# Windowed attention and a gated convolution block on one core: dense stages regrouped from 12 spans of 384 tokens to 9 of 512

## The chip, the core and the metric

One Trainium2 chip, one of its cores. A core has five engines that run their own instruction queues: TensorE (PE in the profile, with its weight loads shown apart as PEld), VectorE (DVE), ScalarE (ACT), GpSimd (POOL) and SyncE (SP), which here only issues transfers (DMA). The engines wait for each other on semaphores. Matrix products go into PSUM, here eight tiles of 128 x 512 float32; everything else lies in SBUF. The metric is the device time of one execution in microseconds, the median of several runs. The profiler gives one execution with every instruction.

## The reference

Eight sequences of 576 tokens, 8 heads of 64. Attention looks at the last 64 tokens only; then a block with a convolution over three neighbouring tokens of a sequence and a sigmoid gate:

```python
scores = scale * np.matmul(q, k.transpose(0, 1, 3, 2))
mask = (rel >= 0) & (rel < window)                  # window = 64
attn = softmax(np.where(mask, scores, -1e9))        # + 1e-9 in the divisor
x = matmul(attn, v)  ->  [8, 576, 512]
h = np.maximum(x @ w_in, 0.0)                       # 512 -> 1024
for k in range(3):
    conv_out += conv_w[k] * hp[:, k:k + S, :]       # hp: h with a zero row at both ends
gate = 1.0 / (1.0 + np.exp(-conv_out))
out = (h * gate) @ w_out                            # 1024 -> 512
```

Inputs q, k, v are float32; the three weights come as float64. All 8 x 576 = 4608 tokens are treated as one row of tokens, cut at the sequence edges only where the window or the convolution asks for it.

## The kernel before

**Tiling.** A span `u` is `NX` = 6 x 64 = 384 tokens, 12 spans. Channels lie on the 128 partitions: 4 tiles of the model width (`NC`), 8 of the inner width (`NF`). Each float32 operand of a dense product is split into a high and a low part in float32r, and each product is three matmuls (high x high, low x high, high x low).

**Attention of a span.** `softmax` works in groups of four blocks of 64 tokens (`NB` = 4), three groups to a span. A group has score matmuls (`qk`, L356) into the two `sc` tiles; `row_max` (L363) on DVE, which adds the mask and finds the maximum; eight `exps` (L373) on ACT; the reciprocal (L379) and `normalise` (L384) on DVE or POOL. The probabilities are then transposed into `ub`: for the first two spans (`BY_PE` = 2) by PE (`transpose_pe` L390, `untile` L395 on ACT), later by DVE (L411) and 12 small transfers per half of a span (`place`, L423). `values` (L495) multiplies them by v for one of four channel tiles into one of the two `acc` tiles; `split_hi` (L499, ACT) and `split_lo` (L502, DVE) write the parts `xh` and `xl`. q, k and v each have one buffer, refilled (L236, L242) when the previous span's products have read it.

**Dense stages of a span.** For each of 8 tiles `f`: `mm1` (L515), 12 matmuls of 384 columns into an `acc` tile, and `relu` (L534 or L538, ACT) into `hbuf`. `hbufs` are two tiles that hold all 8 relu results of a span each. `carry` (L525, POOL) copies the last two columns of the previous span, which the convolution needs. For each pair of tiles: `conv_mid` (L544, ACT), `conv_side` (L551, DVE) for the two neighbours, `sig` (L558, ACT), `gate` (L563, DVE), `gate_hi` (L567, ACT) and `gate_lo` (L571, DVE) into a ring of three `gh`/`gl` tiles. `mm2` (L580) adds, for each `f`, three matmuls into each of the four `po` tiles, which `copy` (L620, L622) brings to `ot` and a transfer (L626; L617 and L624 in the last span) to memory.

**Filler columns.** A sequence of 576 is one and a half spans. Where it ends, in the middle of a span or at its edge, `hbuf` keeps a zero column (L529) between the sequences (`gap_of`), so that the convolution runs over the whole width at once; with the neighbour's column the width is 386 (`NG`) in most spans and 384 in every third but the last. Filler columns go through `mm2` and out to memory, and are dropped on the host.

**The order.** Every piece of work goes into a list by `at(t, engine, cost, ...)`, with a due time `t` in steps (one step: one tile `f`), a cost in microseconds and the keys that it reads and writes. `START` holds the due times, `queued` plays the list on the costs, gives each engine the ready work that is due first, and so fixes the order of each engine's instructions in advance. On the chip each engine then keeps that order. Where PE would wait in the first 110 us, `queued` puts in warm-up matmuls (`keep_busy`, L214). Weights are converted from float64 bits (`to_f32`, L250 to L256; L271 to L274) in the same list, on ACT, DVE and POOL.

Of the kernel before, what the change touches and what calls it, by code (L numbers as in the profile page):

```python
# [15 lines left out]
P = 128  # L16
W = 64
# [5 lines left out]
NT = 6  # L23
NX = NT * W
NU = B * S // NX
NG = NX + 2
NC = DM // P
NF = DFF // P
BY_PE = 2
NB = 4  # L30
NBU = 2 * NT // NB
# [3 lines left out]


LAST = NU - 1


def gap_of(u):  # L40

    return {0: 0, 1: NX // 2, 2: NX}[u % 3]


def width_of(u):
    return NX if u % 3 == 2 and u != LAST else NG

# [11 lines left out]
def queued(works, fill=None):  # L59
# [80 lines left out]
    "v0": -45.616,  # L140
    "pv0": -37.371,
    "conv": -174.861,
    "bits": ((-210.989, -90.898), (-76.132, -86.24)),
    "qk1": -82.37,
    "lag": (5.734, 4.983, 5.01, 5, 4.601, 6.631),
    "mid": (0.325, 6.316, 0.269, 99),
    "v1": -1.517,
    "qk2": -29.766,
    "qk0": (-93.532, -87.041, -82.642),
    "ex0": (-76.037, -72.861, -50.81),  # L150
    "sc1": (-59.709, -43.924, -30.076),
    "ex1": (-36.764, -20.322, -18.147),
    "mask": -51.623,
    "sig": ((5.726, 6.552, 8.72, 10.544), (1.673, 4.482, 8.678, 7.763), (4.834, 5.504, 8.278, 8.811), (4.046, 6.806, 8.285, 10.314)),
    "in": (-91.819, -70.332, -46.356, -13.522, -9.317),
    "out": (5.121, 7.311, 7.45, 11.284),
# [13 lines left out]
def attention_moe(ctx: ExitStack, tc: tile.TileContext, q, k, v, w_in, conv_w, w_out, out):  # L170
# [9 lines left out]
    xh, xl = many(2, [P, NC, NX], F32R, "xh"), many(2, [P, NC, NX], F32R, "xl")  # L180
    hbufs = many(2, [P, NF, NG + 2], F32, "hbuf")
# [9 lines left out]
    ss = many(NBU, [P, NB, 2, P], F32, "s")  # L191
    nms, sms, rs = (many(NBU, [P, 2 * NB], F32, n) for n in ("nm", "sm", "r"))
    cs = many(2, [P, 2, NG], F32, "c")
    ghs, gls = many(3, [P, 2, NG], F32R, "gh"), many(3, [P, 2, NG], F32R, "gl")
# [14 lines left out]
    def keep_busy(n, key):  # L209
        tile = {"sc": sc, "acc": acc, "po": po}[key[0]][key[1]]  # L210

        def do():
            for _ in range(n):
                nc.tensor.matmul(tile[:, 400:], spare, spare[:, :112], start=True, stop=True)  # L214
# [439 lines left out]
    for u in range(NU):  # L654
        n0 = NF * u
        moe(u)
        if u + 1 == NU:
            break
# [92 lines left out]
```

## Time and profile before

| What | us |
|---|---|
| median of 3 runs | 520.48 |
| lowest and highest of them | 519.96, 521.10 |
| the profiled execution | 519.87 |
| its span, first to last instruction | 517.9 |
| busy in the span: PE / DVE / ACT / POOL | 508.0 / 372.4 / 382.8 / 85.4 |

The rows of the profile are read so: engine, line of the kernel, operation, written tile <- read tiles, shapes, count, then busy time and mean nanoseconds of one, then the idle time of the engine before them and what ended it. In timelines and in the chain of waits the first two numbers are start and length in microseconds. In the table of stretches each engine has its busy time and its count of instructions; the three last columns are the granted TensorE clock (1.00 is full), the busy share of the transfer engines and GB/s. A float32 matmul that isn't float32r shows as two rows in the counts (the 576 calls of `values` are 1152 rows).

### The profile page before, as it was taken

The numbers are of one execution on the slowest core, as the hardware profiler recorded it, in microseconds if no ns is written. First come the engines' busy times: TensorE is split into PE (matmuls) and PEld (weight loads), VectorE is DVE, ScalarE is ACT, GpSimd is POOL, SyncE is SP. The second block draws the span as 40 slices with busy tenths as digits, with TensorE's granted clock in tenths as the row PEclk, the third lists the DMA queues.
The fourth block names the chain that finished last, engine by engine and source line by source line (L and its number), as shares of the span: only waits on it lengthen the run. The fifth ranks groups of instructions, "written<-read, shape, count | busy, mean of one in ns | idle before, by whom it ended". The sixth has DMA issues, their size and how long they took to land.

```text
span 517.9 us, 14661 instructions
## 1 busy us (share of the span) xinstructions
PE 508.0 (98%) x5742; PEld 488.4 (94%) x5742; DVE 372.4 (72%) x1084; ACT 382.8 (74%) x1015; POOL 85.4 (16%) x186
## 2 busy tenths in 40 slices
PE   9899899999999999999999999999999999999996
PEld 8788899999999999999899999899899999999996
DVE  4799998986787785766668877677677578554550
ACT  5989797979995894894796895795795696444440
POOL 7123131003030120130121130130130021000000
PEclk9999999999999999999999999999999999999999
DMA  8974923152382461462272451362272043010011
GB/s 294 380 274 171 350 80 117 62 176 76 127 291 69 145 218 47 138 208 66 96 255 60 161 202 49 123 234 55 86 260 65 3 153 121 1 62 2 0 62 61
DMA packets 29460, 69.95 MB, mean 135 GB/s; under 512 B 5712, under 2 KB 17616, under 8 KB 29392
## 3 DMA queue, kind: packets, MB, share of 16 engines
q1 hardware_dynamic: 29392, 69.03, 39.3%
q8 instruction: 45, 0.74, 0.6%
q14 instruction: 23, 0.19, 0.1%
HBM read 47.73 MB, written 9.47 MB: 110 GB/s over the span
## 4 chain that ended last, share of the span: by engine, by line
PE 82%; DVE 9%; DMA 5%; ACT 1%; issue 1%; SPq 1%; ACTq 0%
PE po L580 38%; PE acc L515 33%; PE acc L495 6%; PE sc L356 5%; DMA q<-in_q_dram 2%; DVE s L363 2%; DMA bits<-in_w_out_dram 1%; DVE s L384 1%; DVE T L252 1%; DVE T L256 1%; DMA k<-in_k_dram 1%; DVE c L563 1%; DVE wil L274 1%; DVE xl L502 1%; SPq L236 1%
## 5 line engine op out<-in xcount | busy, mean ns | idle before, releaser
L580 PE MATMUL po<-gh,woh 128*128 128x386 f32 (+1 forms) x384 | 132.4, 345 | 0.0
L515 PE MATMUL acc<-xh,wih 128*128 128x384 f32 x384 | 130.7, 340 | 0.6 <-ACT hbuf L534 0.6
L580 PE MATMUL po<-gh,wol 128*128 128x386 f32 (+1 forms) x384 | 130.0, 339 | 0.0
L580 PE MATMUL po<-gl,woh 128*128 128x386 f32 (+1 forms) x384 | 129.7, 338 | 0.1
L515 PE MATMUL acc<-xh,wil 128*128 128x384 f32 x384 | 129.0, 336 | 0.3 <-issue 0.3
L515 PE MATMUL acc<-xl,wih 128*128 128x384 f32 x384 | 128.8, 335 | 0.0
L551 DVE SCALAR_TENSOR_TENSOR c<-hbuf,cw,c 128x386 f32<-128x386 f32 (+1 forms) x192 | 111.9, 633 | 22.5 <-ACT c L544 22.4
L373 ACT ACTIVATE s<-s,nm 128x96 f32<-128x96 f32 (+2 forms) x288 | 105.1, 368 | 3.4 <-DVE nm L363 3.2
L580 PEld LDWEIGHTS po<-gh,woh 128*128 128x128 f32 x384 | 72.2, 188 | 2.9
L515 PEld LDWEIGHTS acc<-xh,wih 128*128 128x128 f32 x384 | 72.1, 188 | 2.7 <-ACT hbuf L534 1.1
L580 PEld LDWEIGHTS po<-gl,woh 128*128 128x128 f32 x384 | 72.4, 188 | 0.4 <-DVE gl L571 0.4
L515 PEld LDWEIGHTS acc<-xh,wil 128*128 128x128 f32 x384 | 72.1, 188 | 0.5 <-issue 0.5
L580 PEld LDWEIGHTS po<-gh,wol 128*128 128x128 f32 x384 | 72.2, 188 | 0.0
L515 PEld LDWEIGHTS acc<-xl,wih 128*128 128x128 f32 x384 | 72.1, 188 | 0.0
L563 DVE TENSOR_TENSOR c<-c,hbuf 128x772 f32<-128x772 f32 (+1 forms) x48 | 47.0, 982 | 31.2 <-ACT c L558 30.8
L571 DVE TENSOR_TENSOR gl<-c,gh 128x772 fp32r<-128x772 f32 (+1 forms) x48 | 51.8, 1082 | 22.1 <-ACT gh L567 21.8
L384 POOL TENSOR_TENSOR s<-s,r 128x768 f32<-128x768 f32 x27 | 40.4, 1496 | 152.1 <-DVE r L379 138.8
L363 DVE CUSTOM_DVE_ANT_0 s<-sc,mask 128x96 f32<-128x96 f32 (+2 forms) x272 | 51.9, 257 | 16.8 <-PE sc L356 16.8
L373 ACT ACTIVATION_READ_ACCUMULATOR s<-s,nm 128x1 f32 x288 | 54.6, 190 | 0.0
L558 ACT ACTIVATE c<-c 128x772 f32<-128x772 f32 (+1 forms) x48 | 40.6, 847 | 18.8 <-DVE c L551 18.6
L567 ACT CAST gh<-c 128x772 fp32r<-128x772 f32 (+1 forms) x48 | 40.0, 834 | 18.4 <-DVE c L563 13.7
L544 ACT ACTIVATE c<-hbuf,cw 128x386 f32<-128x386 f32 (+1 forms) x96 | 53.5, 608 | 0.0
(63 smaller groups left out, 551.9 us busy)
## 6 DMA issues: line engine op xcount, KB each, us to landing
v<-in_v_dram SPq DMA_DIRECT2D x24, 768.0 KB, 6.4
ub<-T SPq DMA_DIRECT2D x240, 48.0 KB, 1.9
k<-in_k_dram SPq DMA_DIRECT2D x22, 448.0 KB, 6.2
q<-in_q_dram SPq DMA_DIRECT2D x22, 384.0 KB, 7.0
out_dram<-T SPq DMA_DIRECT2D x8, 772.0 KB, 3.8
bits<-in_w_in_dram SPq DMA_DIRECT2D x8, 512.0 KB, 6.1
bits<-in_w_out_dram SPq DMA_DIRECT2D x8, 512.0 KB, 6.6
out_dram<-T SPq DMA_DIRECT2D x3, 768.0 KB, 4.6
```

The lines of the kernel that those rows point to most:

```text
L363: nc.vector.tensor_tensor_reduce(out=ss[b][:, i, h, o:n], in0=banks_of(u, b)[h][:, i * P + o:i * P + n], in1=mask[m][:, o:n], scale=-0.125 ...
L373: nc.scalar.activation(x, x, AF.Exp, bias=nms[b][:, e], scale=-1.0, accum_out=sms[b][:, e])
L384: on.tensor_tensor(sv, sv, rs[b].unsqueeze(2).broadcast_to([P, 2 * NB, n]), ALU.mult)
L495: nc.tensor.matmul(acc[bank(("v", u, c))][h * D:(h + 1) * D, t * W:(t + 1) * W], vs[:, c, t, h], ub[g][:, 2 * p:2 * p + 2, 2 * t + h], sta ...
L515: nc.tensor.matmul(acc[bank(("m", u, f))][:, :NX], w[:, f, c], x[u % 2][:, c], start=(c == 0 and j == 0), stop=(c == NC - 1 and j == 2))
L544: nc.scalar.activation(cs[i % 2][:, a, :n], hbufs[u % 2][:, f, 1:1 + n], AF.Copy, scale=cw[:, 1, f:f + 1])
L551: nc.vector.scalar_tensor_tensor(c, hbufs[u % 2][:, f, e:e + n], cw[:, e, f:f + 1], c, op0=ALU.mult, op1=ALU.add)
L558: nc.scalar.activation(c, c, AF.Sigmoid)
L563: nc.vector.tensor_tensor(c, c, hbufs[u % 2][:, 2 * i:2 * i + 2, 1:1 + n], ALU.mult)
L567: nc.scalar.copy(ghs[ring(u, i)][:, :, :n], cs[i % 2][:, :, :n])
L571: nc.vector.tensor_tensor(gls[ring(u, i)][:, :, :n], cs[i % 2][:, :, :n], ghs[ring(u, i)][:, :, :n].bitcast(F32), ALU.subtract)
L580: nc.tensor.matmul(po[o][:, :n], w[:, f, es], x, start=(f == 0 and j == 0), stop=(f == NF - 1 and j == 2))
```

## The change

- The dense stages go by 9 spans of 512 tokens (`NM` = 2 x 256, `PER` = 2), attention by 18 units of 256 tokens (`NX` = 4 x 64, `NA`). A unit has two groups of four blocks instead of a span's three; the softmax tiles become a ring of three (`NS`).
- Units 0 to 3 (before: spans 0 and 1) are transposed by PE; for units 0 to 3 (before: spans 0 to 2) `normalise` runs on DVE.
- `values` fills an `acc` tile with two channel tiles of 256 tokens, so there are 36 such jobs instead of 48.
- No zero columns: `conv_side` leaves out the column of a neighbour that belongs to another sequence, by cutting the instruction at that place (`spans`). A span is 512 wide, shifted by one column; the last span is 514 and its second product goes in two parts (`parts`), 258 columns into `po` and 256 into halves of the `sc` tiles.
- `hbufs` (two spans of 8 tiles) become `hs`, a ring of `NH` = 5 pairs of tiles.
- `place` moves one group (12 transfers of 32 KB) instead of half a span (12 of 48 KB).
- Costs and due times in `START` are new.

```diff
-NT = 6
+T = B * S
+NT = 4
 NX = NT * W
-NU = B * S // NX
-NG = NX + 2
+NA = T // NX
...
-BY_PE = 2
 NB = 4
-NBU = 2 * NT // NB
+NBU = 2
+NS = 3
+BY_PE = 4
+ON_DVE = 4
+PER = 2
+NU = NA // PER
+LAST = NU - 1
+NM = PER * NX
+NW = NM + 2
+NH = 5
...
-    xh, xl = many(2, [P, NC, NX], F32R, "xh"), many(2, [P, NC, NX], F32R, "xl")
-    hbufs = many(2, [P, NF, NG + 2], F32, "hbuf")
+    xh, xl = many(2, [P, NC, NM], F32R, "xh"), many(2, [P, NC, NM], F32R, "xl")
+    hs = many(NH, [P, 2, NW + 2], F32, "h")
...
+    def ring_of(u, b):
+        return (NBU * u + b) % NS
...
     def values(u, c):
-        g, p = divmod(c, 2)
-        for t in range(NT):
-            for h in range(2):
-                nc.tensor.matmul(acc[bank(("v", u, c))][h * D:(h + 1) * D, t * W:(t + 1) * W], vs[:, c, t, h],
-                                 ub[g][:, 2 * p:2 * p + 2, 2 * t + h], start=True, stop=True)
+        for p in range(2):
+            for t in range(NT):
+                for h in range(2):
+                    nc.tensor.matmul(acc[bank(("v", u, c))][h * D:(h + 1) * D, p * NX + t * W:p * NX + (t + 1) * W],
+                                     vs[:, 2 * c + p, t, h], ub[c][:, 2 * p:2 * p + 2, 2 * t + h], start=True, stop=True)
...
     def mm1(u, f, half):
         for c in (2 * half, 2 * half + 1):
             for j, (w, x) in enumerate(((wih, xh), (wil, xh), (wih, xl))):
-                nc.tensor.matmul(acc[bank(("m", u, f))][:, :NX], w[:, f, c], x[u % 2][:, c],
+                nc.tensor.matmul(acc[bank(("m", u, f))], w[:, f, c], x[u % 2][:, c],
                                  start=(c == 0 and j == 0), stop=(c == NC - 1 and j == 2))
...
+    def slot(u, i):
+        return (NF // 2 * u + i) % NH
+
+    def carry(u, i):
+        h = hs[slot(u, i)]
         if u == 0:
-            nc.gpsimd.memset(hbuf[:, fs, :2], 0.0)
+            nc.gpsimd.memset(h[:, :, :2], 0.0)
         else:
-            e = NX if (u - 1) % 3 == 2 else NX + 1
-            nc.gpsimd.tensor_copy(hbuf[:, fs, :2], hbufs[(u - 1) % 2][:, fs, e:e + 2])
...
+            nc.gpsimd.tensor_copy(h[:, :, :2], hs[slot(u - 1, i)][:, :, NM:NM + 2])
...
+    def spans(u, e):
+
+        n, t0, res = width_of(u), u * NM - 1, [0]
+        for j in range(n):
+            if 0 < t0 + j < T - 1 and (t0 + j) % S == (0 if e == 0 else S - 1):
+                res += [j, j + 1]
+        res.append(n)
+        return [(x, y) for x, y in zip(res[::2], res[1::2]) if y > x]
...
+    def parts(u, o):
+
+        if u != LAST:
+            return [(0, NM, po[o][:, :NM], halves_of("po", o))]
+        n = NM // 2
+        return [(0, n + 2, po[o][:, :n + 2], halves_of("po", o)),
+                (n + 2, NW, sc[o // 2][:, o % 2 * n:(o % 2 + 1) * n], halves_of("sc", 0)[o // 2:o // 2 + 1])]
...
-                at(t + 0.05, "SP", 2.1, lambda g=g, i=i: place(g, i), r=[("T", g)], w=[("u", g, i)], mb=0.15)
+            at(t + 0.05, "SP", 1.35, lambda i=i: place(b, i), r=[("T", b)], w=[("u", b, i)], mb=0.1)
...
+    "qk": ((-198.384, -170.949), (-193.671, -162.337), (-154.854, -108.704), (-106.623, 1.483), (-6.498, -3.826), (1.331, 4.543), (-0.713, -0.42), (3.501, 3.738)),
+    "ex": ((-164.895, -164.822), (-138.633, -119.099), (-52.881, -37.596), (2.064, 5.523), (1.401, -2.24), (5.799, 5.838), (-0.443, 0.159), (4.214, 4.945)),
+    "pv": ((-139.987, -153.554), (-84.882, -86.539), (1.278, 4.685), (5.77, 6.895), (4.8, 6.129), (7.71, 7.584), (3.763, 3.861), (7.594, 7.387)),
```

381 lines of the change are left out of this document (160 added, 221 removed), and 4 rows, old and new, of the table START.

## The prediction

> **What bounds the kernel now.** I read the page first: shares of the engines, the slices, the chain that ended last.
>
> ```profile
> span 517.9 us, 14661 instructions
> PE 508.0 (98%) x5742; PEld 488.4 (94%) x5742; DVE 372.4 (72%) x1084; ACT 382.8 (74%) x1015; POOL 85.4 (16%) x186
> ...
> PEclk9999999999999999999999999999999999999999
> ...
> PE 82%; DVE 9%; DMA 5%; ACT 1%; issue 1%; SPq 1%; ACTq 0%
> ```
>
> TensorE (PE) is busy for 98% of the span at the full granted clock, and 82% of the chain lies on it. A busy matmul row isn't a full array, so I went on to the table of stretches, for whether other engines are close behind, and to PE's timeline for the first dense matmul.
>
> ```profile
> 34.90:67.00 32.10, 30.53 (x487) 27.86 (x485) 31.34 (x94) 28.82 (x71) 10.06 (x19) 1.00 0.69 257
> 340.00:380.00 40.00, 40.00 (x481) 38.68 (x480) 28.66 (x89) 30.42 (x83) 6.51 (x12) 1.00 0.38 126
> ...
> 34.88 0.42 PE L515 MATMUL acc<-xh,wih 128*128 128x384 f32 x1
> ...
> 513.50 0.34 PE L580 MATMUL po<-gl,woh 128*128 128x386 f32 x1
> ```
>
> The columns are the stretch, its length, then busy time of PE, PEld, DVE, ACT and POOL. In the steady part VectorE (28.66 of 40) and ScalarE (30.42) have a quarter of their time free, while PE has none. From 34.88, the first dense matmul, to 513.50, the last one, lie 478.6 us in which PE hardly stops. So the time is a start of 34.9, plus 478.6 of PE work, plus 4.4 of result copies and transfers up to 517.9. The profiled execution took 519.87, 2.0 beyond its span; the median of the three runs is 520.48. My sum is made against 519.87. About 0.2% (1 us) is what a measurement of this kernel can tell from no change.
>
> **The dense matmuls (the main term).** What one costs is read from the chain in order of time (start, length, what).
>
> ```profile
> 482.12 2.10 PE acc L515 x12
> ...
> 496.89 16.96 PE po L580 x96
> ```
>
> ```profile
> L515 PE MATMUL acc<-xh,wih 128*128 128x384 f32 x384 | 130.7, 340 | 0.6 <-ACT hbuf L534 0.6
> L580 PE MATMUL po<-gh,woh 128*128 128x386 f32 x288 | 99.2, 344 | 0.0
> L580 PE MATMUL po<-gh,woh 128*128 128x384 f32 x96 | 33.2, 346 | 0.0
> ...
> L515 PEld LDWEIGHTS acc<-xh,wih 128*128 128x128 f32 x384 | 72.1, 188 | 2.7 <-ACT hbuf L534 1.1
> ```
>
> From one to the next it is 2.10 / 12 = 175 ns for a first product (384 columns) and 16.96 / 96 = 176.7 ns for a second one (386). There are 3 x 384 of each: 1152 x 0.175 + 1152 x 0.1767 = 405.2 us. The change keeps the columns (it drops the fillers: 9 x 386 + 3 x 384 = 4626 become 4610 per weight tile) and cuts the instructions: 9 spans x 96 = 864 first products of 512, 8 x 96 = 768 second ones of 512, and 192 of about 257 in the last span, whose 514 columns don't fit a po tile of 512.
>
> How much of the 175 ns goes by the instruction? No row shows another width of this kind of matmul. A weight load is busy for 188 ns although pairs follow each other every 175, so about 13 ns of each load lie beyond the step from pair to pair; I take this as the hand-over that each instruction pays once. The rest is 162 / 384 = 0.422 ns a column (0.424 for the second). Then 512 columns take 229 and 230 ns and 257 take 122: 864 x 0.229 + 768 x 0.230 + 192 x 0.122 = 198.0 + 176.7 + 23.4 = 398.0, that is -7.2 us. One end: all of it goes by columns, 512 take 233 ns, and only the fillers are saved, -0.7. The other end is a line through the nearest narrow row, the warm-up matmuls:
>
> ```profile
> 12.04 3.60 PE L214 MATMUL acc<-spare 128*128 128x112 f32 x30
> ```
>
> These take 120 ns at 112 columns, so (175 - 120) / 272 = 0.20 ns a column, 201 ns at 512, 149 at 257, and some -47 us. I don't believe it: a 112-column matmul is more likely paced by its weight load of 128 columns than by itself. I take 229.
>
> The Trainium skill, "TensorE: Matmul & The Clock Gate", section "Back-to-back issue gap", gives N/2.4 + 2.5 ns for a warm isolated gap: 162.5 at 384, where this trace has 175, and 216 at 512. An estimate by that page alone would make the saving of fixed time 480 fewer instructions x 2.5 ns = 1.2 us, which speaks against the change; the trace's 12 ns more are not explained by it.
>
> **Attention on PE.** The work per token stays, its grouping changes.
>
> ```profile
> 31.78 1.62 PE L495 MATMUL acc<-ub,v 128*64 128x64 f32 x48
> ...
> 39.25 1.04 PE L390 MATMUL po<-ident,s 128*128 128x128 f32 x8
> ```
>
> ```profile
> 404.48 0.33 PE L580 MATMUL po<-gl,woh 128*128 128x384 f32 x1
> 404.74 1.62 PE L495 MATMUL acc<-ub,v 128*64 128x64 f32 x48
> 406.29 1.00 PE L356 MATMUL sc<-k,q 64*32 64x96 f32 x64
> 407.21 0.44 PE L580 MATMUL po<-gh,woh 128*128 128x384 f32 x1
> 407.50 0.34 PE L580 MATMUL po<-gh,wol 128*128 128x384 f32 x1
> ```
>
> (a) Four units of 256 are transposed by PE instead of two of 384: 8 groups, not 6. Four of them, not two, come after the first dense matmul: 2 more x 1.04 = +2.1. Those before it displace warm-up matmuls, at nothing. (b) Scores: 36 groups of about 0.95 as before, 32 rather than 30 behind the start, +2; values: the first 128 of 1152 instructions rather than 96 come before it, -1.0; a DVE transpose and a placing fall away for units 2 and 3. Since a group of unit 2 can be computed before the start, as the plan's due times have it, I take +0.7 together. (c) Each change between dense and small matmuls costs PE 0.26 - 0.175 going in and 0.29 - 0.175 coming out, 0.2 us. The value products stand in blocks of 48 (two together); behind the start there are 1056 / 48 = 22 such blocks. After, 32 products make 16 blocks if each pair stays together, as their due times lie 0.1 and 0.2 of a step apart, 32 if none does: -1.2 to +2.0; I take -1.2.
>
> **Vector and scalar work** is the same per column in fewer, longer instructions; the cuts at the sequence edges add 7 edges x 2 sides x 8 tiles = 112 small VectorE instructions. Both lie in the 10 of 40 us that VectorE has free. If that cover goes (34.90 to 67.00, where DVE is busy for 31.34 of 32.10), each costs its time.
>
> **The ring of five** makes a relu wait until the pair five before has been gated. Before, all 8 tiles of the previous span stay. Run-ahead is longest at the start:
>
> ```profile
> 34.88:66.77 31.89, 21.78 (x114) 19.47 (x114) 1.00 0.69 258
> ...
> 34.88:66.77 31.89, 1.83 (x2) 1.00 0.69 258
> ```
>
> The first row counts first products, the second the gate multiplications in the same stretch: 114 x 384 columns, as many as 85 x 512, 7.1 tiles or under 4 pairs; the ring holds 5. Cost nothing; if gating stood still for 10 us more, the ring would end first.
>
> ```profile
> L384 POOL TENSOR_TENSOR s<-s,r 128x768 f32<-128x768 f32 x27 | 40.4, 1496 | 152.1 <-DVE r L379 138.8 <-ACT xh L499 10.7 <-ACT c L544 2.5
> L525 POOL COPY hbuf<-hbuf 128x4 f32<-128x4 f32 x44 | 21.7, 493 | 181.4 <-ACT hbuf L538 95.2 <-ACT hbuf L534 86.1
> ```
>
> The carry on GpSimd now guards a slot that the next pair overwrites; it is a 0.5 us copy that can queue behind a 1.5 us normalisation, but is due some two tiles (over 10 us) ahead.
>
> **The start.** The first dense matmul now needs 512 tokens, i.e. four groups of scores instead of three, and values of two units that share one v buffer.
>
> ```profile
> 19.96 0.92 PE L495 MATMUL acc<-ub,v 128*64 128x64 f32 x24
> ...
> 23.04 0.33 SPq L242 DMA_DIRECT2D v<-in_v_dram  x1
> ```
>
> ```profile
> 0.00:34.88 34.88, 15.23 (x77) 1.00 0.86 310
> ...
> v<-in_v_dram SPq DMA_DIRECT2D x24, 768.0 KB, 6.4
> ...
> L499 ACT CAST xh<-acc 128x384 fp32r<-128x384 f32 x48 | 22.4, 476 | 17.8 <-PE acc L495 17.4
> L502 DVE TENSOR_TENSOR xl<-acc,xh 128x384 fp32r<-128x384 f32 x48 | 26.2, 555 | 8.8 <-ACT xh L499 7.6
> ```
>
> The 77 rows are exponentials and their sums on ScalarE: 38, almost five groups of eight, were done by 34.88, and four are needed after. Values of unit 0 around 20 to 22, its buffer reloaded (6.4), values of unit 1 at 28 to 30, a split of 512 columns ((0.476 + 0.555) x 1.33 = 1.4): 31 at the earliest. One group later at ScalarE's pace (15.23 / 38 x 8 = 3.2, with copies some 4): 39. I take 34.9, no change, between 31 and 39.
>
> **The end**: the last bank is again copied in two pieces, so 4.4 stays.
>
> Sum: -7.2 + 2.1 + 0.7 - 1.2 = -5.6; 519.87 - 5.6 = **514.3 us**.
>
> **Rivals.**
> 1. *The time goes by columns.* -0.7 in place of -7.2: 520.8, no change. For it: no row shows another width. Against it: the 13 ns of the weight load. Chance 0.10. By the rule of the Trainium skill named above ("TensorE: Matmul & The Clock Gate", 2.5 ns fixed) the time would come out here too, 0.5 lower.
> 2. *SyncE's queue becomes the bound: slower.* Placing a group issues 12 small transfers, whatever its length.
>
> ```profile
> 305.50 12.65 SPq L423 DMA_DIRECT2D ub<-T  x18
> ...
> ub<-T SPq DMA_DIRECT2D x240, 48.0 KB, 1.9
> k<-in_k_dram SPq DMA_DIRECT2D x22, 448.0 KB, 6.2
> ...
> 330.41 0.33 SPq L236 DMA_DIRECT2D k<-in_k_dram  x1
> ...
> L373 ACT ACTIVATE s<-s,nm 128x96 f32<-128x96 f32 x240 | 86.9, 366 | 0.2
> L373 ACT ACT_TABLE_LOAD x18 | 23.1, 1283 | 4.3 <-DVE nm L363 4.1
> L411 DVE STREAM_TRANSPOSE T<-s 128x768 f32<-128x768 f32 x20 | 19.4, 971 | 3.4 <-POOL s L384 3.3
> ```
>
> 12.65 / 18 = 0.70 us each, 8.4 a group. After, 28 groups issue 336 (of 32 KB), 48 in a dense span of about 52 us: 34 us of SP's time, before 17 of 40. The scores of a span's second unit are due 4.2 steps into it and its values at 7.4: 3.2 steps of 52 / 8 = 6.5, 20.6 us. Eight exponentials with a table load 2.9 + 1.3 = 4.2, normalising 1.5, transposing 1.0, two placings 16.9, landing 1.9: 25.5. It decides if an issue takes over about 0.50 us. The following first products then find no input, and PE's order is fixed: if half of the 4.9 us shows in each of 8 spans, +20, **534**. If the issue goes by bytes (0.47), 19.9 fits. A load of 448 KB that issues in 0.33 speaks against a cost by bytes; later dense work queued ahead of the values can absorb some. Chance 0.13.
> 3. *A late start.* First products at 41 in place of 34.9, because loads and weight conversions compete with the fourth group: 520.4. Against it: five groups were done by then before. Chance 0.10.
> 4. *More gain.* A start at 31 and whole pairs: down to 507, chance 0.09; a matmul halfway between my 229 ns and the 201 of the line through the warm-up row, 215, takes 1632 x 0.014 = 23 more off: 491, chance 0.03.
>
> **How the numbers follow.** Forecast 508 to 518.5, chance 0.55. Rival 2 and the far part of 4 (0.16) stay out of the range, the others are in: 507 to 523. Rivals 1 and 3 lie around the time before: of each 0.02 is faster, 0.06 within 0.2%, 0.02 slower. Faster by over 0.2%: 0.55 + 0.12 + 0.04 = 0.71. Within: 0.12. Slower: 0.13 + 0.04 = 0.17.
>
> **What would show it.** Twelve first products in 2.75 us in the chain (2.80 says rival 1); the first dense matmul between 31 and 39; PE without gaps to the end; 16 blocks of 64 value matmuls. Waits of value products for "ub", and SP's queue full, say rival 2. I am wrong if PE's rows after 60 us show idle time in every span.

## The result and the profile after

The changed kernel took **536.61 us** (median; 534.59 to 538.55) beside 520.79 us for the kernel before on the same chip: a ratio of 1.031 with a 95% interval of 1.026 to 1.035, slower. 514.3 was forecast, within 507 to 523. The profiled execution took 537.26 us, 17.4 more than the 519.87 against which the sum was made.

The page of the kernel after (span; busy time by engine; granted clock by slice; the chain that ended last, by engine):

```profile
span 535.5 us, 13610 instructions
...
PE 509.1 (95%) x5180; PEld 418.7 (78%) x5180; DVE 368.5 (69%) x1096; ACT 375.9 (70%) x932; POOL 76.6 (14%) x122
...
PEclk8999999999899999999999998999999999999999
...
PE 72%; DVE 12%; DMA 4%; SPq 4%; ACT 4%; issue 3%; POOL 0%; ACTq 0%; POOLq 0%
...
ub<-T SPq DMA_DIRECT2D x336, 32.0 KB, 1.9
```

PE was busy for 98% of a span of 517.9 before, now for 95% of 535.5, and its share of the chain fell from 82 to 72%. In its place stand DMA, SyncE's queue (SPq, which issues the transfers) and "issue", time in which an engine waits for nothing that the profile shows. The placing transfers (ub<-T) rose from 240 to 336, each two thirds as large. What PE waited for is told by its table of waits (tile and line that waited, releaser: us in all, times, longest):

```profile
PE acc L452 <- DMA ub<-T: 8.5, 4, 3.1
PE sc L339 <- issue: 4.6, 4, 2.2
...
PE acc L452 <- issue: 0.6, 1, 0.6
```

Value products waited four times, 8.5 us, for the placing transfers. Score products stood still four times, 4.6 us, without a releaser. (Waits for loads of q, not shown, lie before the first dense product.) Here is one of each in PE's timeline (start, length, what, count, the idle time before), with SyncE's queue beside the first:

```profile
115.01 16.45 SPq L392 DMA_DIRECT2D ub<-T  x24
```

```profile
128.08 0.64 PE L339 MATMUL sc<-k,q 64*32 64x96 f32 x32
129.17 0.69 PE L452 MATMUL acc<-ub,v 128*64 128x64 f32 x16 [0.46 <-DMA ub<-T]
132.96 0.56 PE L452 MATMUL acc<-ub,v 128*64 128x64 f32 x5 [3.10 <-DMA ub<-T]
```

```profile
326.24 0.96 PE L339 MATMUL sc<-k,q 64*32 64x96 f32 x61
329.40 0.53 PE L339 MATMUL sc<-k,q 64*32 64x96 f32 x3 [2.19 <-issue]
329.86 0.80 PE L552 MATMUL po<-gh,woh 128*128 128x512 f32 x1
330.45 0.63 PE L552 MATMUL po<-gh,wol 128*128 128x512 f32 x1
330.88 0.63 PE L552 MATMUL po<-gl,woh 128*128 128x512 f32 x1
...
332.58 0.47 PE L552 MATMUL po<-gh,woh 128*128 128x512 f32 x1
```

SyncE issues 24 transfers from 115.01 to 131.46, 0.69 us each though they carry 32 KB and not 48; the value products that need the last of them start at 132.96. The second pause has no such cause, and the dense products behind it follow each other at 427 ns (330.45, 330.88): six steps from 329.86 to 332.58 take 2.72 us where 233 ns each would be 1.40. The granted clock by stretch shows the two places where that happened (length, busy time by engine, PEclk):

```profile
100.00:140.00 40.00, 34.29 (x366) 27.88 (x365) 30.87 (x97) 34.31 (x94) 6.25 (x6) 0.91 0.46 128
140.00:300.00 160.00, 155.76 (x1676) 126.19 (x1682) 106.58 (x343) 109.66 (x266) 20.20 (x22) 1.00 0.40 123
300.00:340.00 40.00, 37.81 (x389) 30.32 (x367) 26.02 (x89) 27.70 (x75) 5.84 (x6) 0.96 0.50 146
```

The start, the end, and the pace of the dense products, from timeline and chain (in the chain's row: start, length, line, count):

```profile
38.12 0.47 PE L477 MATMUL acc<-xh,wih 128*128 128x512 f32 x1
...
529.52 0.28 PE L552 MATMUL sc<-gl,woh 128*128 128x256 f32 x1
```

```profile
417.03 5.61 PE acc L477 x24
...
501.24 2.82 PE po L552 x12
```

So the 17.4 us are: start +3.2 (38.12 against 34.88), end +1.6 (6.0 after the last matmul against 4.4), waits for ub +8.5, pauses without releaser +5.2 (4.6 of scores, 0.6 of values), slow clock twice 1.3. That is 21.1; the remainder, -3.7, is what the regrouping of the small products and the dense steps save less what the transposes add. The dense products, from which -7.2 were expected, saved next to nothing: 5.61 / 24 = 233.7 ns a step in the row above. On the mean over the kernel after, slow clock aside, 864 x 233.4 + 768 x 233.0 + 192 x 119.5 ns = 403.5 us, where 1152 x 174.8 + 1152 x 176.3 ns = 404.5 us stood before: about -1 us.

### The profile page after: what moved, and what is told of

The parts are those of the page before. It is cut to its first block, busy times and chain, and to the rows that moved or that the text cites. A ratio compares the mean times of both kernels' runs of the same rounds, so it can differ in the third digit from the quotient of the medians.

```text
span 535.5 us, 13610 instructions
## 1 busy us (share of the span) xinstructions
PE 509.1 (95%) x5180; PEld 418.7 (78%) x5180; DVE 368.5 (69%) x1096; ACT 375.9 (70%) x932; POOL 76.6 (14%) x122
## 4 chain that ended last, share of the span: by engine, by line
PE 72%; DVE 12%; DMA 4%; SPq 4%; ACT 4%; issue 3%; POOL 0%; ACTq 0%; POOLq 0%
PE po L552 30%; PE acc L477 27%; PE acc L452 5%; PE sc L339 5%; SPq L392 4%; DVE c L515 3%; PE sc L552 2%; DMA q<-in_q_dram 2%; ACT s L357 2%; DVE s L346 2%; PE acc L205 2%; DVE gl L535 2%; DVE c L527 1%; DMA bits<-in_w_in_dram 1%; DVE T L241 1%
## 5 line engine op out<-in xcount | busy, mean ns | idle before, releaser
L515 DVE SCALAR_TENSOR_TENSOR c<-h,cw,c 128x512 f32<-128x512 f32 (+29 forms) x256 | 115.9, 517 | 34.5 <-ACT c L499 34.5
L477 PE MATMUL acc<-xl,wih 128*128 128x512 f32 x288 | 114.4, 397 | 0.0
L477 PE MATMUL acc<-xh,wih 128*128 128x512 f32 x288 | 114.0, 396 | 0.0
L477 PE MATMUL acc<-xh,wil 128*128 128x512 f32 x288 | 113.7, 395 | 0.0
L552 PE MATMUL po<-gh,woh 128*128 128x512 f32 (+1 forms) x288 | 112.4, 390 | 0.2 <-issue 0.2
L552 PE MATMUL po<-gh,wol 128*128 128x512 f32 (+1 forms) x288 | 111.4, 387 | 0.0
L552 PE MATMUL po<-gl,woh 128*128 128x512 f32 (+1 forms) x288 | 110.8, 385 | 0.0
L346 DVE CUSTOM_DVE_ANT_0 s<-sc,mask 128x96 f32<-128x96 f32 (+2 forms) x280 | 54.2, 258 | 33.5 <-PE sc L339 33.3
L535 DVE TENSOR_TENSOR gl<-c,gh 128x1024 fp32r<-128x1024 f32 (+1 forms) x36 | 44.6, 1248 | 18.0 <-ACT gh L531 17.8
L527 DVE TENSOR_TENSOR c<-c,h 128x1024 f32<-128x1024 f32 (+1 forms) x36 | 47.7, 1324 | 13.1 <-ACT c L522 13.0
L499 ACT ACTIVATE c<-h,cw 128x512 f32<-128x512 f32 (+1 forms) x72 | 47.9, 714 | 3.7 <-DVE gl L535 3.5
```

Source lines behind the costliest of these rows:

```text
L346: nc.vector.tensor_tensor_reduce(out=ss[ring_of(u, b)][:, i, h, o:n], in0=banks_of(u, b)[h][:, i * P + o:i * P + n], in1=mask[m][:, o:n], ...
L477: nc.tensor.matmul(acc[bank(("m", u, f))], w[:, f, c], x[u % 2][:, c], start=(c == 0 and j == 0), stop=(c == NC - 1 and j == 2))
L499: nc.scalar.activation(cs[i % 2][:, a, :n], hs[slot(u, i)][:, a, 1:1 + n], AF.Copy, scale=cw[:, 1, f:f + 1])
L515: nc.vector.scalar_tensor_tensor(c, hs[slot(u, i)][:, a, e + x:e + y], cw[:, e, f:f + 1], c, op0=ALU.mult, op1=ALU.add)
L527: nc.vector.tensor_tensor(c, c, hs[slot(u, i)][:, :, 1:1 + n], ALU.mult)
L535: nc.vector.tensor_tensor(gls[ring(u, i)][:, :, :n], cs[i % 2][:, :, :n], ghs[ring(u, i)][:, :, :n].bitcast(F32), ALU.subtract)
```

## The experiments

Two questions: what makes the pauses, and why did the dense step not fall below 233 ns? **Theory B**: value products wait because SyncE's queue needs 0.69 us a placing transfer whatever its size, while the program's order was worked out with 1.35 us for three. **Theory C1**: a run of more than some 380 PE instructions without dense work (score, value and score products, with the weight loads 64 x 3 x 2 = 384) outruns the fetching of PE's own instructions; the rival **C2** is an unseen wait elsewhere. **Theory A**: a dense product's time goes by its columns; against it stands the prediction's 13 ns + 0.422 ns a column.

### The pauses

**place_one**: two thirds of the placing transfers left out.

```
     def place(g, i):
-        for j in range(3):
+        for j in range(1):
```

> As after, but each placing group issues 4 of its 12 transfers of the transposed probabilities and leaves the others out, so two thirds of the values' weights are missing; the order of everything else on each engine is that of after. Theory B (SyncE's queue, at 0.65 us a transfer, makes the value products late): the waits of the value products for ub (8.5 us, 4 places) fall under 1 us, the slow stretch of the clock after 129.6 us goes with them, and the time is 9 to 12 us less (525 to 528 us). Theory C (the loss is in the score groups' own gaps, marked issue): those stay (5 us in the gaps and 1.5 us of slow clock), and the time falls by less than 3 us.

519.67 us, 0.998 of before (0.997 to 1.000): 17 us less than after. PE's waits:

```profile
PE sc L339 <- issue: 2.4, 2, 1.5
```

No row for ub is left. The gain is larger than the 9 to 12 expected, since two of the four pauses of the scores (2.2 us) and both slow stretches (2.6) went too. That a wait for ub delays is shown; that it is the issuing isn't, as the transfers are gone as well.

**place_true**: the planner that orders the instructions is told what a placing step takes.

```
-            at(t + 0.05, "SP", 1.35, lambda i=i: place(b, i), r=[("T", b)], w=[("u", b, i)], mb=0.1)
+            at(t + 0.05, "SP", 2.0, lambda i=i: place(b, i), r=[("T", b)], w=[("u", b, i)], mb=0.1)
```

> As after, but the planner that fixes the order of the instructions counts 2.0 us for a placing step (3 transfers at 0.67 us, as the trace has them) in place of 1.35 us. Theory B (the order is built on a placing queue that is faster than the real one): value products are put later, the waits for ub fall from 8.5 us to under 3 us, and the time by 5 to 10 us (527 to 532 us). Rival (the queue is too slow for the work whatever the order): the waits remain or move to the later stages or to the end, 534 to 540 us.

524.71 us, 1.010 (1.007 to 1.012): 12 us come back with all 336 transfers in place. So the queue isn't too slow for the work; the order had been laid out for a faster one. PE's waits have no row for ub, and two pauses remain:

```profile
PE sc L339 <- issue: 2.4, 2, 1.4
```

It is better than the 527 to 532 expected: the later values also part most of the long runs, of which PE's timeline has four left in place of eleven (192 small products without a dense one).

**place_pool**: every third transfer is issued by GpSimd, in the order of after.

```
-            nc.sync.dma_start(ub[g][o:o + HW, i], tbuf[HW * i:HW * (i + 1), g, j])
+            (nc.gpsimd if j == 2 else nc.sync).dma_start(ub[g][o:o + HW, i], tbuf[HW * i:HW * (i + 1), g, j])
```

> As after, but every third placing transfer (j = 2) is issued by GpSimd's queue, so that SyncE has 8 in place of 12 a group, 5.4 us at 0.67 us each; the program's order is that of after. Theory B (SyncE's queue is what the value products wait for, and its time goes by the number of transfers, not by the bytes): the waits for ub fall from 8.5 us to under 2 us, the slow clock after 129.6 us goes, 521 to 527 us. Rival 1 (the transfers themselves, not their issue, are late): the waits stay within 2 us, 534 to 538 us. Rival 2 (GpSimd issues slowly and holds VectorE up): new waits on VectorE's softmax, 530 to 540 us.

523.13 us, 1.005 (1.003 to 1.008). The waits for ub are gone, with the same bytes landing and SyncE's share of the issues cut by a third: it is the issuing through SyncE (the engine and the queue behind it were not parted). Theory B holds. What is left are two pauses without releaser, with the slow clock behind one of them:

```profile
PE sc L339 <- issue: 3.3, 2, 2.1
```

```profile
300.00:340.00 40.00, 37.78 (x330) 30.40 (x329) 26.04 (x74) 25.69 (x58) 10.81 (x18) 0.96 0.32 90
```

**split_both**: the last two pairs of the scores' due times (START, "qk") are moved apart, so that dense work parts the long runs.

```
...
-(-0.713, -0.42), (3.501, 3.738)),
+(-1.15, -0.1), (2.9, 4.05)),
```

> As after, but two pairs of due times of the score products are moved apart ((-0.713, -0.42) and (3.501, 3.738) become (-1.15, -0.1) and (2.9, 4.05)), so that dense work stands between the blocks: no block of score, value and score products in a row (384 PE instructions with the weight loads) is left, the longest has score and value products only (256). Four more switches between dense and small work for each such block cost about 0.2 us each, 3 us in all. Theory C1 (long runs of small products outrun the fetching of PE's instructions): the gaps marked issue inside the score groups at 245.7, 327.0, 357.1 and 438.0 (5.5 us) vanish, and the slow clock behind 327 (1.4 us) with them; the waits for ub stay: time 531 to 535 us. Theory C2 (the gaps come with the fetch wherever it falls): they move elsewhere, time 536 to 540 us.

531.61 us, 1.022 (1.018 to 1.027), within the expected range. No pause stands inside the score products any more; value products wait as before, and 0.9 us without releaser are among them:

```profile
PE acc L452 <- DMA ub<-T: 6.8, 6, 2.2
...
PE acc L452 <- issue: 0.9, 2, 0.8
```

**C1 by itself.** The stream kernel **widths** (its other half is read below) ends with 384 products of the scores' shape, so 768 instructions with the weight loads (half as many products as its expectation says). PE has nothing to wait for there; VectorE is still multiplying until 194.9:

```
+        for n in (512, 128, 192, 256, 320, 384, 448, 512):
+            stream(n)
...
+        for r in range(6):
...
+                            nc.tensor.matmul(sc[h][o:o + HW, i * P:i * P + KW], xf[hs, p, t:t + HW], wf[hs, p, t:t + KW], start=True, stop=True)
```

> The kernel computes nothing of the reference: it runs streams of 96 float32r products (8 groups of 12) at 128, 192, 256, 320, 384, 448 and 512 columns with the other engines idle, then 256, 384 and 512 while VectorE and ScalarE work, and then 768 small float32 products (64x32x96) in one run. Theory A (a dense product's time goes by its columns: 175 ns at 384 and 233 ns at 512 in the kernel after): the steps lie on one line through nearly zero, 512 at 4/3 of 384 within 2% (about 233 and 175), 256 near 119. Theory of the prediction (a fixed 13 ns each plus 0.422 ns a column): 512 near 229, 256 near 121, and 128 near 67 instead of 58. Theory A2 (the columns cost 0.42 ns by themselves, and other engines' use of the memories stretches the wide ones): idle 512 near 220 or less, and 4 to 8% more in the busy streams. Theory C1 (a long run of small products outruns the fetching of PE's instructions): within the 768 small products there are gaps of 1.5 to 2.5 us, one about every 250 to 400 instructions with their weight loads; theory C2 (the gaps of the kernel after come from another wait): no gap over 0.3 us in them.

PE's timeline at that place, and the row of its instruction queue in the page (transfers, MB):

```profile
188.63 2.44 PE L206 MATMUL sc<-wf,xf 64*32 64x96 f32 x191
192.93 1.71 PE L206 MATMUL sc<-wf,xf 64*32 64x96 f32 x128 [1.85 <-issue]
196.38 1.00 PE L206 MATMUL sc<-wf,xf 64*32 64x96 f32 x65 [1.74 <-issue]
```

```profile
q8 instruction: 12, 0.20, 0.3%
```

PE stops after 191 products (382 instructions) and again after 128 (256). The whole kernel's 3072 PE instructions came in 12 transfers of about 16 KB, 256 instructions each. The run uses 256 instructions in 1.71 us, but the next 256 start only 3.45 us after them (192.93 to 196.38). The trace also has the time of each of these transfers. Here two land at 191.52 and 194.85, and PE goes on 1.4 and 1.5 us later. In the kernel after, blocks land at 246.06, 328.07, 356.33 and 437.41, and the four pauses of the scores end 1.3 to 1.5 us behind them (247.32, 329.40, 357.78, 438.77); the two pauses each of place_one, place_true and place_pool end 1.4 to 1.6 us behind one. So C1 is shown, in the kernel too, and C2 is not needed for these pauses; the 0.6 us of a value product (0.9 in split_both) has no such transfer beside it and stays open. Length alone is not the rule: place_true's second pause comes after 59 score products, with only six dense products between them and 128 small ones. A dense product (two instructions in 233 ns) uses a block in 30 us. The Trainium skill, "Runtime: NRT & Kernel Launch", section "Instruction fetch mechanics", describes the refill in 16 KiB blocks of 256 instructions, and calls its cost mostly hidden; the block's size agrees with these rows, and the hiding holds for dense products but not for a long run of small ones.

**true_split** and **pool_split** join both cures: place_true or place_pool with split_both's due times.

> As place_true with the due times of split_both: value products ordered for placing at 2.0 us a step, and no score, value and score blocks in a row. Theories B and C1 together: of place_true's remaining gaps marked issue (236.9 and 400.4 us, 2.9 us with 320 ns taken off each) both vanish, the waits for ub stay under 1 us, and some ten more switches between dense and small work cost 0.2 us each: 522 to 525 us, within 0.5% of place_true. If the blocks' lengths do not matter, the gaps move and the time is 525 to 528 us.

524.61 us, 1.009 (1.007 to 1.011), level with place_true. The pauses without releaser vanished, but two waits for ub came back:

```profile
PE acc L452 <- DMA ub<-T: 3.3, 2, 2.2
```

The scores' due times shift the values' too. It is a tie that tells little by itself.

> As after with both edits: every third placing transfer on GpSimd's queue, and the due times of split_both. Theories B and C1: neither waits for ub nor gaps inside the score groups; what is left against before is the start (+3.2 us), the end (+1.6 us), transposes and the like (+3.1 us) and two or three us of switches won: 521 to 525 us, about 1.005 of before. If place_pool's rival 2 holds: 530 us or more.

**519.89 us, 0.999 (0.998 to 1.001): level with before**, 1 us better than expected. Neither kind of pause is left, and PE has the chain again (page); the longest row of its waits is VectorE's, as short as in the other runs:

```profile
PE 94%; DVE 3%; DMA 2%; issue 0%; SPq 0%; ACT 0%
```

```profile
PE sc L339 <- DVE nm L346: 2.0, 5, 0.5
```

**before_pool**: the kernel before with every third placing transfer on GpSimd.

> The kernel before with every third placing transfer (j = 2) on GpSimd's queue, order unchanged. Its value products hardly wait for ub (stalls of 0.6 us in all over the span), so theory B expects no gain: 519.5 to 521.5 us, ratio 0.998 to 1.002. If it gains over 1.5 us, SyncE's queue held the kernel before as well, and the change with the same edit is not level with it.

520.46 us, 1.001 (0.999 to 1.002). The queue did not hold the kernel before; what the edit gains in the kernel after mends a fault that the change brought with it.

### The dense step

**widths** first. The stretches each hold 96 steps with the other engines idle (in the last one VectorE and ScalarE work), at 256, 384, 448, 512 and 512 columns (stretch, its length, PE, PEld, DVE, ACT, POOL, PEclk):

```profile
54.68:66.22 11.54, 11.54 (x99) 11.54 (x98) 0.00 (x0) 0.00 (x0) 0.00 (x0) 1.00 0.01 1
80.30:96.94 16.64, 16.64 (x98) 16.64 (x97) 0.00 (x0) 0.00 (x0) 0.00 (x0) 1.00 0.00 0
96.94:116.78 19.84, 19.84 (x98) 18.02 (x98) 0.00 (x0) 0.00 (x0) 0.00 (x0) 1.00 0.00 1
116.78:138.58 21.80, 21.80 (x97) 18.02 (x96) 0.00 (x0) 2.45 (x3) 0.00 (x0) 1.00 0.00 1
166.74:188.54 21.80, 21.80 (x97) 17.84 (x96) 21.21 (x18) 12.90 (x13) 0.00 (x0) 1.00 0.00 1
```

Divided by 96: 120.2, 173.3, 206.7, 227.1 and 227.1 ns. The rise from 256 to 384 and on to 512 columns is 0.42 ns a column, and 12 to 14 ns are fixed: the prediction's line, to within 2 ns. At 448 columns a step lies some 6 ns above the straight line between 384 and 512; no run tells why, so the line holds for the widths that the kernels use and not for every one. At 128 columns a step still takes 111 ns. Theory A, which would have 231 at 512, falls for a stream alone. But in the kernel after, 1578 steps at 512 columns take 233.2 on the mean. (The Trainium skill, "TensorE: Matmul & The Clock Gate", section "Back-to-back issue gap", has N/2.4 + 2.5 for an isolated product, that is 162.5 and 215.8 at 384 and 512 columns; the runs show 11 ns more at both, so its slope agrees and its fixed part does not for these products.)

**widths2**: the same at 512 and 384 columns, beside loads from HBM, PSUM reads by VectorE and ScalarE, GpSimd, and then with the kernel's pattern of three products, over two and over four banks.

```
+        for i in range(24):
+            nc.sync.dma_start(lf[i % 2], q[i % NA])
+        for n in (512, 384):
+            stream(n)
...
+            for i, (w, x) in enumerate(((wh, xh), (wl, xh), (wh, xl))):
```

> The kernel computes nothing of the reference: streams of 96 float32r products (8 groups of 12) at 512 and 384 columns, one pair idle, one under loads from HBM, one while VectorE and ScalarE read PSUM, one while GpSimd multiplies in SBUF, one with the kernel's three products from two halves of weights and activations, and one with these rotating over four PSUM banks. Known: 227.1 and 173.4 ns alone (widths), 233.1 and 174.8 in the kernels. Theory A (the prediction's line of 13 ns + 0.422 ns a column holds for a stream alone, and something that runs beside it in the kernel takes 6 ns of a wide step and 1.4 of a narrow one): the stream beside which the 512 step rises to 231 to 237 names it, and the 384 step rises there by under 3 ns. Theory A2 (it is the kernel's own pattern, two tiles for each operand): the last pairs show 233 and 175 with all else idle. If all stay within 1 ns of 227, neither is shown and the 6 ns stay open.

All five at 512 columns took 21.80 us for 96 steps, with loads at 261 GB/s (first row) as without anything (second, the three products):

```profile
74.37:96.17 21.80, 21.80 (x97) 18.03 (x97) 0.00 (x0) 0.00 (x0) 0.00 (x0) 1.00 0.82 261
...
189.77:211.57 21.80, 21.80 (x97) 18.03 (x97) 0.00 (x0) 0.00 (x0) 0.00 (x0) 1.00 0.00 0
```

Neither neighbours nor the pattern: a miss that leaves the place of the operands.

**widths3**: activations and weights in five places of the memory each.

> The kernel computes nothing of the reference: streams of 96 float32r products at 512 columns with the activations in five places of the memory some 26 KB apart, the weights in five places, the activations 8 and 32 bytes off, the results over four PSUM banks, and one stream at 386 columns. Known: 227.1 ns alone, 233.1 in the kernels, and neither neighbours nor the pattern of operands gave the 6 ns. If the place of an operand costs them, some of the streams show 231 to 237 ns; if all stay at 227, the 6 ns of a wide step stay open.

Behind the first, which meets the slow clock, every stream at 512 columns took 230.9 to 233.4 ns, and the one at 386 took 177.0. Nothing ran beside. By the addresses in the programs, the operands' tiles begin 32 bytes beside a multiple of 64 here, and on one in widths and widths2; in the kernel after the weights begin at 62752, 32 bytes beside one, in the kernel before at 62848, on one. So four kernels move the weights:

```
     hs = many(NH, [P, 2, NW + 2], F32, "h")
+    pool.tile([P, 8], F32, name="gap")
```

> As after, with 32 bytes left free in each partition ahead of the four weight tiles, so that they begin on a multiple of 64 bytes as they did before (62848) and as in widths and widths2; in after (62752) and in widths3 they begin 32 bytes beside one. Theory W (a wide dense product whose weights lie 32 bytes off takes 231 to 237 in place of 227 ns): first products at 512 columns fall from 233.3 to 227 to 229 ns, second ones too if the weights alone decide, 864 x 5.5 = 4.8 to 1632 x 6 = 9.8 us less; the waits for ub and the issue gaps stay or grow a little, since the order was planned without it: 527 to 533 us. Rival (the place has nothing to do with it): steps stay at 233, 535 to 538 us.

> pool_split with the same 32 bytes: no stalls are left in it that could take the gain back. Theory W: 519.9 - 4.8 = 515.1 down to 519.9 - 9.8 = 510.1 us, faster than both kernels by 1 to 2%. Rival: 519 to 521 us.

> best_w with the rows of the gated activations (gh, gl) padded from 514 to 528 numbers, so that every one begins on a multiple of 64 bytes; in after and best_w half of them begin 8 or 32 bytes beside. If the activations' place matters as the weights' does, the second products (768 at 512 columns) fall by a further 2 to 6 ns: 1.5 to 4.5 us less than best_w. If the weights alone decide: within 1 us of best_w.

> The kernel before with 32 bytes put ahead of its weight tiles, so that these begin 32 bytes beside a multiple of 64, as in after. Theory W: its first products (384 columns, 174.8 ns) rise towards the 177 ns that widths3 shows at 386, 1152 x 2 = 2.3 us, and the second ones (386 columns, 176.5 ns) by 0 to 2 ns: 521.5 to 526 us, ratio 1.003 to 1.011. Rival: 519.5 to 521.5 us.

w64 took 533.35 us (1.024, 1.021 to 1.027), best_w 517.46 (0.994, 0.992 to 0.995), best_wg 515.23 (0.990, 0.988 to 0.991), before_w32 519.85 (0.999, 0.997 to 1.000). So w64 ends just above its range, best_w between theory and rival, and best_wg 2.2 us below best_w, as expected. The steps at 512 columns fell from 233.2 to 231.3, 231.2 and 230.2 ns. So places matter, but theory W brings only half of what it promised, and before_w32 misses altogether: no rise at 384 columns. In best_wg the second products gained when their activations moved, so it isn't the weights alone.

**widths4** moves one operand by a few bytes at a time, both based on a multiple of 64.

```
+                nc.tensor.matmul(acc[g % 2][:, :n], w[:, ws:ws + P], x[:, xs:xs + n], start=(j == 0), stop=(j == 11))
...
+        for xo, wo, n in ((0, 0, 512), (0, 0, 512), (0, 2, 512), (0, 8, 512), (0, 16, 512), (0, 32, 512), (0, 64, 512), (8, 0, 512),
+                          (16, 0, 512), (32, 0, 512), (64, 0, 512), (128, 0, 512), (2, 0, 512), (8, 8, 512), (0, 0, 384), (0, 8, 384), (8, 0, 384)):
```

> The kernel computes nothing of the reference: streams of 96 float32r products at 512 columns, with weights (w) and activations (x) each in one tile that begins on a multiple of 64 bytes, and the slices moved by 8, 32, 64, 128 or 256 bytes, one at a time; at last three streams at 384 columns. Theory W (weights 32 bytes off a multiple of 64 make a 512-column product slower): 227 ns with w at 0, 64, 128 and 256 bytes, 231 to 237 at 32 (and 8), whatever x does. Theory X (the activations' place decides): 227 at x 0, 64, 128, 256, and 231 to 237 at 8 and 32. Both may hold, as best_wg suggests (3 of the 6 ns came back). At 384 columns 173.4 in all three, as before_w32 suggests. If all are 227, it is not the multiple of 64.

Stretches of 96 steps each (the first three numbers are all that is read): weights at 0, 32, 128 and 256 bytes with the activations at 0; activations at 32 with weights at 0; both at 32; and, at 384 columns, weights at 0 and at 32.

```profile
30.76:52.52 21.76, 21.76 (x97) 18.02 (x96) 0.00 (x0) 0.00 (x0) 1.00 0.00 0
...
74.67:97.07 22.40, 22.40 (x97) 18.04 (x96) 0.00 (x0) 0.00 (x0) 1.00 0.00 1
...
119.47:141.77 22.30, 22.30 (x97) 18.09 (x96) 0.00 (x0) 0.00 (x0) 1.00 0.00 0
141.77:163.53 21.76, 21.76 (x97) 18.02 (x96) 0.00 (x0) 0.00 (x0) 1.00 0.00 1
163.53:185.94 22.41, 22.41 (x98) 18.00 (x97) 0.00 (x0) 0.00 (x0) 1.00 0.00 1
296.14:317.94 21.80, 21.80 (x98) 18.03 (x97) 0.00 (x0) 0.00 (x0) 1.00 0.00 0
317.94:334.58 16.64, 16.64 (x98) 16.64 (x96) 0.00 (x0) 0.00 (x0) 1.00 0.00 1
334.58:351.22 16.64, 16.64 (x97) 16.64 (x97) 0.00 (x0) 0.00 (x0) 1.00 0.00 1
```

Both theories fall as put. A multiple of 64 isn't enough (128 bytes: 22.30 / 96 = 232.3 ns), and an odd place does no harm if both operands share it (both at 32: 227.1). In these streams what decides is whether weights and activations **stand alike within 256 bytes**, that is, whether their addresses leave the same remainder when divided by 256: alike 227, unlike 229 to 233. At 384 columns 32 bytes make no difference (173.3), which is why before_w32 showed none. widths3 fits in: its two rows of activations lie 2112 bytes apart, 64 beyond a multiple of 256, so no stream there has both alike with the weights; the four with one of the two alike take 230.9 ns, the others 231.6 to 233.3. In after, xh and xl stand at 128 beyond a multiple of 256, the weights at 32.

**best_w256** and **best_256** carry the rule into pool_split: 96 bytes before the weights bring them to 128 as well; best_256 does so for gh and one of the three gl tiles too (there was no room for the other two, called gm).

```
+    pool.tile([P, 24], F32, name="gap")
...
-    ghs, gls = many(3, [P, 2, NW], F32R, "gh"), many(3, [P, 2, NW], F32R, "gl")
+    pool.tile([P, 16], F32, name="gap2")
+    ghs = many(3, [P, 2, NW + 62], F32R, "gh")
+    gls = many(1, [P, 2, NW + 62], F32R, "gl") + many(2, [P, 2, NW], F32R, "gm")
```

> pool_split with 96 bytes free ahead of the weight tiles, so that weights (62848) and activations (xh 9344, xl 25728) both stand at 128 beyond a multiple of 256 bytes; widths4 shows 227 ns where the two stand alike within 256 bytes and 229 to 233 where not. First products at 512 columns fall from 233.4 (pool_split) and 230 (best_w, 64 against 128) to 227, 864 x 6.4 = 5.5 us less than pool_split; second products, whose gated rows still begin anywhere, stay at 231 to 233: 513 to 515.5 us. Rival (the rule of the streams does not carry over to the kernel): 517 to 520 us.

> best_w256 with the rows of gh (and of one of three gl tiles) padded to 576 numbers and begun at 128 beyond a multiple of 256 bytes as well; memory has no room for the other two gl tiles. Some 7 in 9 of the second products then stand alike with their weights: 768 x 7/9 x 5 = 3 us less than best_w256, 510 to 512.5 us, about 0.983 of before, without a change in the order of the program. Rival: within 0.5 us of best_w256.

best_w256: 516.27 us (0.992, 0.991 to 0.994), a little short of the gain expected (513 to 515.5), with the first products at 228.4 ns and the second still at 233. best_256: **512.72 us, 0.985 of before (0.984 to 0.987)**, the fastest of all and 0.2 above its range. Twenty-four first and twelve second products in its chain:

```profile
420.29 5.45 PE acc L480 x24
...
477.21 2.77 PE po L555 x12
```

5.45 / 24 = 227 ns where after had 233.7. On the mean over the kernel the first products take 227.9 ns and the second 229.3, so that all dense steps come to 396.0 us, 8.5 less than before. The control lies inside the kernel: from start to start, second products that read the aligned gl tile take 227.5 ns (69 of them), those that read gm 231.3 (128).

## Why the prediction was wrong, step by step

**What failed.** The sum let PE run behind the start without a wait, and two causes broke that: value products waited for ub, which the prediction had priced as a rival and left out of its range, and PE's own instructions came late, which it did not have at all. Together with the slow clock behind two of these stops they are 8.5 + 5.2 + 2.6 = 16.3 of the 17.4 us. The other step that failed is the size of the main term: -7.2 forecast, about -1 measured.

**The dense matmuls (-7.2).** The fixed part and the slope were right for a stream alone, the term came out as about -1. Thirteen ns of fixed time and 0.422 ns a column is what streams show, 227 where 229 was taken. What the step left out is where tiles lie: new tile sizes put the weights at 62752 where 62848 stood before, and a product of 512 columns pays up to 6 ns for that, one of 384 nothing. Rival 1's price was thus nearly right, and its reason (time by columns) wrong. With most operands alike, best_256 has the term back: -8.5. The choice of 229 over the 201 of the line through the warm-up row held: that row is narrower than 192 columns, and from 128 to 192 a step stays at 111 to 112 ns in widths.

**Rival 2** is what mainly happened, at 0.13: place_pool, which takes its wait away, is 13.5 us faster than after (the slow clock behind the wait included). That its 534 is near 536.61 is luck, as it had 20 us of waits and nothing lost on the dense steps. It was priced from the right row: 0.70 us an issue then, 0.69 after, beyond the 0.50 from which it was to decide. I had even named the load of 448 KB that issues in 0.33 us against a cost by bytes, and still gave the rival little. Its heading was wrong, though: the queue isn't the bound. SyncE issues the same 336 transfers in place_true, 12 us faster. What was late is the fixed order, in which value products stood ahead of their data. The waits came at four places, with dense work queued behind them, 8.5 us in all (9.8 with the slow clock behind one) and not in every span as priced.

**A cause that the prediction lacked**: PE's own instructions. Fewer and larger blocks of small products, which the step on switches counted as a gain, make runs of 384 instructions. The pauses of the scores (4.6 us) and the slow clock after one of them (1.3) were the price. The switches themselves gained more than the -1.2: PE's rows have 20 blocks of small products behind the start in place of 36, as score products were joined to the value products too. From the first dense product to the last, the dense rows take 5.2 us less of PE's time with the slow clock left aside; about 1 of it is their steps, some 4 are the switches.

**Transposes (+2.1)**: +1.7 in PE's rows. **Scores and values (+0.7)**: not to be told apart from the pauses. **Start (0)**: +3.2, within the bounds of 31 to 39; what of it the fourth group of scores takes, no run shows. **End (0)**: +1.6; why the copies and transfers after the last matmul take 6.0 us, no run shows. **Ring of five, vector and scalar work (0)**: right; no row of the waits names the ring, and PE's waits for VectorE's maxima are 1.5 us where 1.3 stood before.

Without pauses, slow clock and the lost term the time comes out beside the forecast: best_256 at 512.72. In part that is luck. Its dense steps give 8.5 us where 7.2 were forecast, its start (38.86) and its end (5.5) take 5.1 us more where 0 was forecast, and small products 2.9 us shorter and shorter waits (1.0) make up for much of that.

## What to carry to other kernels

The placing transfers cost SyncE 0.70 us each at 48 KB and 0.69 at 32 KB: a price by the piece. Whoever makes such tiles smaller makes more pieces, and a planner that scales their price with the bytes lays out an order that waits. Joining small matmuls into long runs saves switches until the run is longer than the instructions at hand (382 here): part it with dense work. And when a change of tile sizes is timed, look at where the tiles now lie, before the step of the main matmul is explained by its shape.

## What the runs showed of the hardware that was not expected

- A float32r product of 128x128 by 512 columns takes 227 ns in widths4 if weights and activations stand alike within 256 bytes, 229 to 233 if not, and up to some 237 in the kernel after (the products of xl); at 384 columns 173.3 with and without 32 bytes between them. Why, no run shows.
- PE ran out of instructions after 382 in a row at 6.4 ns each (2.44 us / 382), and then got 256 in 3.45 us. In every pause of the scores it went on 1.3 to 1.6 us after a transfer of instructions had landed.
- An idle time of 2.19 us (329.40) was followed by six dense steps at about 427 ns; one of 2.81 us for ub at 187.68 was not, as the clock of 1.00 from 140 to 300 shows. So length alone does not decide. The Trainium skill, "TensorE: Matmul & The Clock Gate", section "What's actually happening", tells of a free-running window of about 3.4 us; that fits a pause that matters only by where it falls, but no run here shows the window, and a pause of 2.19 us is shorter than it.
- GpSimd issued a placing transfer in 0.51 us (row below, pool_split), SyncE in 0.69. Little of that came back through VectorE's softmax: PE waited 2.0 us for L346 in pool_split, 1.5 in place_one.

```profile
L392 POOL DMA_DIRECT2D ub<-T x112 | 56.8, 510 | 72.8 <-issue 50.4
```
